# Two long-lived buffer pools of an attention and gated-MLP kernel change places in SBUF

## The chip, the core and the metric

The kernel runs on one core of one Trainium2 chip. The metric is device time in microseconds (us) of one execution, lower is better. The kernel before the change took 1835.28 us (median of 3 runs, 1833.83 to 1836.11).

## The reference

Three layers in a row on 4,608 tokens of width 512, all in float32. First an attention whose keys and values are averaged over groups of 8 positions, then a gated MLP, then an MLP with a rational function in place of the usual activation:

```
k_p, v_p = mean over groups of 8 rows of k, v            # 576 -> 72 per head
attn     = softmax(q @ k_p.T / 8);  x = attn @ v_p        # 8 batches, 8 heads, 64 wide
g        = x @ w_gate;  y = (silu(g) * (x @ w_val)) @ w_out      # 512 -> 1536 -> 512
h        = y @ w_in                                       # 512 -> 2048
P        = a0 + a1 h + a2 h^2 + a3 h^3
Q        = 1 + |b0| |h| + |b1| h^2
out      = (P / (Q + 1e-6)) @ w_out2                      # 2048 -> 512
```

## The kernel before, in words

A float32 operand is kept as two halves, a rounded `fp32r` part and the remainder, 512 columns each, side by side in one tile of 4,096 bytes a partition. A product is then three matmuls of 128x128 by 128x512 into one PSUM bank: high by high, low by high, high by low (`mm3`, L256, and the loop at L1081). Every matmul has a weight load of its own (a 128x128 stationary operand) in front of it, which TensorE runs while the matmul before it streams its 512 columns (the moving operand).

Tokens are worked on in nine blocks of 512. The work has four stages:

1. Blocks 0 to 2 of the gated MLP, a block for each outer turn (`gp` and `vp`: weights stationary, tokens `x` moving; `acc`: `w_out` stationary, the hidden tile `ht` moving). Attention for the blocks to come is put in between. In the first turn the weights are still being converted from their raw form.
2. Blocks 3 to 8 in three pairs, by a scheme of seven products in place of eight (`ca`, `cb`, `cc`, 36 turns). Weights and weight sums are streamed from HBM into slots (`sw`), the tokens' sums and differences lie in slots too (`x0t`, `x0b` and so on).
3. The output product of these pairs (L1081, `ya`, `yb`, `yc`). The weights (`oa`, `os`) lie in slots. The moving tiles go round a ring of seven: four tiles of the long-lived pool, then three slots (`ring_tile`).
4. The second MLP (L1110 on): 9 blocks of 16 turns. In a turn twelve matmuls `h` (weights `wi` stationary, tokens `z` moving) and then twelve matmuls `acco` of the turn two before (hidden tile `gt` stationary, weights `wo` moving). Of the token tiles `z` those of even blocks lie in slots and those of odd blocks in the long-lived pool (the last argument of `convert_x`).

The order of the instructions on each engine is written out by hand (`manual_schedule`); the pools decide addresses only. A tile pool takes the next free bytes of each partition when it is opened, so the order in which pools are opened sets where they lie. Two pools matter here:

- `wp`: 36 slots of 4,096 bytes, 147,456 bytes in all, a multiple of 256 (`wslot`).
- `keep`: five small tiles (`ident`, `vmask`, `cab`, `neg`, `lnb`), which take 640 bytes together, then four token tiles `x0` to `x3` of 4,096 bytes and `xraw` of 8,192 bytes.

The pools that are opened later (`hp` with `ht`; in the second MLP `p2` with `gt`) begin behind both.

Of the kernel before, what the change touches and what calls it, by code (L numbers as in the profile page):

```python
# [63 lines left out]
def attention_gated_rational(  # L64
# [3 lines left out]
):  # L68
    nc = tc.nc
    ctx.enter_context(tc.manual_schedule())  # L70
    wp = ctx.enter_context(tc.tile_pool(name="wp", bufs=WSLOTS))
    keep = ctx.enter_context(tc.tile_pool(name="keep", bufs=1))
    dram = ctx.enter_context(tc.tile_pool(name="dram", bufs=1, space=DRAM))
    ps_acc = ctx.enter_context(tc.tile_pool(name="ps_acc", bufs=4, space=PSUM))
    ps_gv = ctx.enter_context(tc.tile_pool(name="ps_gv", bufs=2, space=PSUM))
# [1162 lines left out]
```

## Time and profile before

| | |
|---|---|
| median of 3 runs | 1835.28 us |
| span of the profiled execution | 1834.7 us |
| TensorE matmul busy | 1772.9 us (97%) |
| VectorE busy | 1403.0 us (76%) |
| ScalarE busy | 1135.3 us (62%) |
| GpSimd busy | 342.8 us (19%) |
| matmuls of 128x512 | 7,020 of 8,212 |

The span is from the first to the last instruction of one profiled execution. The engine names of the rows are PE (TensorE matmul), PEld (TensorE weight load), DVE (VectorE), ACT (ScalarE), POOL (GpSimd) and SP (SyncE). The duration of one matmul in the profile (some 390 ns) runs from its start to its modelled end and overlaps the next one; what one costs in a stream is the distance between starts. Where a text speaks of the pitch, it means that distance: the time from the start of one run of matmuls to the start of the next, over their number.

### The profile page before, as it was taken

What the parts mean: (1) busy time and instruction counts of PE and PEld (TensorE: products, weight loads), DVE (VectorE), ACT (ScalarE), POOL (GpSimd) and SP (SyncE); (2) the same over time, 40 slices, a digit from 0 to 9 for tenths busy, and PEclk for the clock granted to TensorE, in tenths of its full rate; (3) what the DMA queues carried; (4) which work ended last, traced back from release to release, by engine and by line L of the source; (5) the groups of instructions that cost most, each with busy time, mean ns of one, the idle gap of its engine ahead of it and who ended that gap; (6) DMA issues with size and microseconds to landing.
All of it is one profiled execution on the core that took longest, in us unless ns stands there. A gap on an engine that the chain in (4) does not pass through costs nothing.

```text
span 1834.7 us, 23841 instructions
## 1 busy us (share of the span) xinstructions
PE 1772.9 (97%) x8212; PEld 1425.9 (78%) x8212; DVE 1403.0 (76%) x2333; ACT 1135.3 (62%) x1994; POOL 342.8 (19%) x492
## 2 busy tenths in 40 slices
PE   5899999999999999999999999999999999999998
PEld 4677877787777788777888788888888888888887
DVE  6996665558678666546777898889888989898987
ACT  5676455547665665435455666676667766776675
POOL 2343555442354344210000000000000000000000
PEclk9999999999999999999999999999999999999999
DMA  6531756659999788999826601010101010101000
GB/s 248 207 115 51 236 168 233 195 183 330 353 327 346 281 327 294 326 364 362 318 106 229 241 1 46 1 46 1 46 1 46 1 46 1 46 1 46 1 24 23
DMA packets 157464, 285.27 MB, mean 155 GB/s; under 512 B 12320, under 2 KB 78496, under 8 KB 156320
## 3 DMA queue, kind: packets, MB, share of 16 engines
q1 hardware_dynamic: 156624, 283.43, 44.1%
q8 instruction: 65, 1.06, 0.2%
q10 hardware_dynamic: 720, 0.33, 0.1%
q14 instruction: 55, 0.45, 0.1%
HBM read 194.58 MB, written 89.13 MB: 155 GB/s over the span
## 4 chain that ended last, share of the span: by engine, by line
PE 61%; DMA 1%; DVE 1%; ACT 0%; issue 0%; POOL 0%; SPq 0%; DVEq 0%; ACTq 0%
PE acco L256 22%; PE h L256 21%; PE ya L1081 5%; PE ca L256 4%; PE yc L1081 3%; PE cc L256 2%; PE yb L1081 1%; PE cb L256 1%; DMA sw<-wd 0%; DMA hl<-h 0%; PE pv L457 0%; DMA os<-so 0%; POOL t L722 0%; PE sc L368 0%; DVE gt L1169 0%
## 5 line engine op out<-in xcount | busy, mean ns | idle before, releaser
L256 PE MATMUL acco<-wo,gt 128*128 128x512 f32 x1728 | 426.6, 395 | 2.7 <-ACT gt L1168 2.2
L256 PE MATMUL h<-z,wi 128*128 128x512 f32 x1728 | 422.5, 393 | 0.0
L256 PEld LDWEIGHTS acco<-wo,gt 128*128 128x128 f32 x1728 | 324.9, 188 | 80.9 <-ACT gt L1168 3.1
L256 PEld LDWEIGHTS h<-z,wi 128*128 128x128 f32 x1728 | 324.3, 188 | 75.7
L1147 ACT ACTIVATE sq<-h 128x512 f32<-128x512 f32 x144 | 86.1, 598 | 221.6 <-PE h L256 221.4
L1154 DVE SCALAR_TENSOR_TENSOR w<-sq,neg,w 128x512 f32<-128x512 f32 x144 | 108.2, 751 | 66.9 <-ACT w L1148 62.4
L256 PE MATMUL vp<-x,wv 128*128 128x512 f32 x432 | 111.7, 406 | 5.9 <-DVE wv L149 5.9
L1164 DVE SCALAR_TENSOR_TENSOR g<-t,neg,e 128x512 f32<-128x512 f32 x144 | 108.2, 752 | 5.1
L1151 ACT ACTIVATE t<-h,neg 128x512 f32<-128x512 f32 x144 | 112.0, 778 | 0.0
L256 PE MATMUL gp<-x,wg 128*128 128x512 f32 x432 | 109.4, 400 | 2.6 <-DVE wg L149 2.6
L1160 DVE SCALAR_TENSOR_TENSOR t<-t,neg,h 128x512 f32<-128x512 f32 x144 | 107.7, 748 | 5.1
L1161 DVE SCALAR_TENSOR_TENSOR e<-w,ln 128x512 f32<-128x512 f32 x144 | 98.7, 686 | 13.5 <-ACT ln L1158 13.4
L256 PE MATMUL acc<-ht,wo 128*128 128x512 f32 x432 | 107.5, 398 | 0.0
L1158 ACT ACTIVATE ln<-ln,lnb 128x512 f32<-128x512 f32 x144 | 104.2, 724 | 4.7
L1162 DVE SCALAR_TENSOR_TENSOR e<-e,ln 128x512 f32<-128x512 f32 x144 | 99.7, 692 | 5.0
L1168 ACT ACTIVATE gt<-g 128x512 fp32r<-128x512 f32 x144 | 91.0, 632 | 16.8 <-DVE g L1164 16.8
L256 PEld LDWEIGHTS vp<-x,wv 128*128 128x128 f32 x432 | 81.0, 192 | 26.2 <-DVE wv L149 8.5
L1169 DVE TENSOR_TENSOR gt<-g,gt 128x512 fp32r<-128x512 f32 x144 | 98.8, 686 | 1.5 <-ACT gt L1168 0.8
L1148 ACT ACTIVATE w<-h,cab 128x512 f32<-128x512 f32 x144 | 98.3, 683 | 2.5 <-DVE e L1161 2.4
L1159 DVE TENSOR_TENSOR t<-t,h 128x512 f32<-128x512 f32 x144 | 98.2, 682 | 0.0
L256 PEld LDWEIGHTS gp<-x,wg 128*128 128x128 f32 x432 | 79.4, 188 | 23.3 <-DVE wg L149 4.7
L256 PEld LDWEIGHTS acc<-ht,wo 128*128 128x128 f32 x432 | 81.2, 190 | 18.5
(247 smaller groups left out, 3164.1 us busy)
## 6 DMA issues: line engine op xcount, KB each, us to landing
sw<-sd SPq DMA_DIRECT2D x72, 512.0 KB, 7.4
sw<-wd SPq DMA_DIRECT2D x36, 512.0 KB, 5.9
h<-hq SPq DMA_DIRECT2D x36, 512.0 KB, 6.5
sd<-sp SPq DMA_DIRECT2D x24, 512.0 KB, 4.1
sw<-vd SPq DMA_DIRECT2D x36, 256.0 KB, 7.7
hl<-h SPq DMA_DIRECT2D x18, 512.0 KB, 7.0
hr<-h SPq DMA_DIRECT2D x18, 512.0 KB, 9.9
out<-ob SPq DMA_DIRECT2D x36, 256.0 KB, 2.4
```

Of the source, the lines that this page charges most:

```text
L256: nc.tensor.matmul(acc, st[:, lw, cols], mv[:, rw, mcols], start=first and i == 0, stop=last and i == n - 1, skip_group_check=seeded,)
L1081: nc.tensor.matmul(banks[q], w[:, lw, cols], t[:, rw, :], start=opened and k == 0 and m == 0, stop=k == NK - 1 and m == 2, skip_group_chec ...
L1148: nc.scalar.activation(w0, hps, AF.Abs, scale=cab[:, 4:5])
L1151: nc.scalar.activation(t, hps, AF.Identity, scale=neg[:, 3:4], bias=neg[:, 2:3])
L1154: nc.vector.scalar_tensor_tensor(w0, sq, neg[:, 5:6], w0, op0=ALU.mult, op1=ALU.add)
L1158: nc.scalar.activation(ln, ln, AF.Exp, scale=-1.0, bias=lnb)
L1159: nc.vector.tensor_tensor(t, t, hps, op=ALU.mult)
L1160: nc.vector.scalar_tensor_tensor(t, t, neg[:, 1:2], hps, op0=ALU.add, op1=ALU.mult)
L1161: nc.vector.scalar_tensor_tensor(e, w0, C1, ln, op0=ALU.add, op1=ALU.mult)
L1162: nc.vector.scalar_tensor_tensor(e, e, 2.0, ln, op0=ALU.subtract, op1=ALU.mult)
L1164: nc.vector.scalar_tensor_tensor(g, t, neg[:, 0:1], e, op0=ALU.add, op1=ALU.mult)
L1169: lambda gt=gt, g=g: nc.vector.tensor_tensor(gt[:, 1, :], g, f32(gt[:, 0, :]), op=ALU.subtract),
```

## The change

Two lines change places, so that `keep` is opened first and `wp` second:

```diff
     nc = tc.nc
     ctx.enter_context(tc.manual_schedule())
+    keep = ctx.enter_context(tc.tile_pool(name="keep", bufs=1))
     wp = ctx.enter_context(tc.tile_pool(name="wp", bufs=WSLOTS))
-    keep = ctx.enter_context(tc.tile_pool(name="keep", bufs=1))
     dram = ctx.enter_context(tc.tile_pool(name="dram", bufs=1, space=DRAM))
```

No instruction is added, removed or moved: the order on all five engines is the same in both programs, row for row. What differs is the byte of a partition at which tiles begin, here in the built programs:

| tiles | before | modulo 256 | after | modulo 256 |
|---|---|---|---|---|
| slots of `wp` | 1,152 + 4,096 i | 128 | 26,368 + 4,096 i | 0 |
| `x0` to `x3` of `keep` | 149,248 + 4,096 i | 0 | 1,792 + 4,096 i | 0 |
| `xraw` of `keep` | 165,632 | 0 | 18,176 | 0 |
| `ident` of `keep` | 148,608 | 128 | 1,152 | 128 |
| `ht` and `cq` | 188,160 and 192,256 | 0 | the same | 0 |
| `gt` (second MLP) | 186,112 and 190,208 | 0 | the same | 0 |
| all other tiles of later pools | from 173,824 on | | the same | |

The low half of a pair begins 2,048 bytes into its tile, and a stationary operand is cut out of its tile at multiples of 512 bytes, so both halves and all cuts of a tile have the tile's byte modulo 256. Before the change a matmul's two operands so begin either at the same byte modulo 256 (slot with slot), or 128 bytes apart (slot with anything else). After it all 7,020 matmuls of 128x512 have both operands at 0 modulo 256. The smaller matmuls of the attention have operands in pools that don't move, but for block 0, whose attention tiles lie in slots.

## Rows read from the trace of the kernel before

**Rows 1.** The page: span, and busy time of each engine.

```profile
span 1834.7 us, 23841 instructions
PE 1772.9 (97%) x8212; PEld 1425.9 (78%) x8212; DVE 1403.0 (76%) x2333; ACT 1135.3 (62%) x1994; POOL 342.8 (19%) x492
```

**Rows 2.** Stretches: attention start, first MLP's three blocks, pairs, their output, second MLP.

```profile
core 0: us, PE busy (x) PEld busy (x) DVE busy (x) ACT busy (x) POOL busy (x), PEclk, DMA share, GB/s
39.70:176.80 137.10, 122.29 (x580) 93.83 (x579) 125.23 (x219) 98.71 (x164) 55.63 (x57) 0.98 0.33 114
176.80:293.60 116.80, 114.98 (x573) 92.71 (x573) 72.57 (x137) 55.95 (x107) 62.39 (x103) 1.00 0.63 202
293.60:424.00 130.40, 127.94 (x692) 102.30 (x691) 72.35 (x137) 66.21 (x101) 62.95 (x104) 1.00 0.63 211
424.00:848.80 424.80, 409.82 (x2025) 328.44 (x2024) 269.57 (x525) 246.54 (x468) 149.90 (x207) 0.99 0.94 332
848.80:1025.00 176.20, 174.63 (x757) 141.82 (x756) 131.37 (x215) 88.72 (x156) 0.00 (x0) 1.00 0.68 241
1025.00:1834.67 809.67, 803.33 (x3457) 649.03 (x3455) 706.03 (x1042) 559.03 (x935) 0.00 (x0) 1.00 0.08 29
```

**Rows 3.** What TensorE waited for in the whole span: us in total, times, longest.

```profile
PE vp L256 <- DVE wv L149: 5.9, 6, 1.8
PE t L429 <- POOL p L404: 5.8, 4, 2.2
...
PE ca L256 <- DMA sw<-wd: 2.7, 2, 1.8
PE gp L256 <- DVE wg L149: 2.6, 5, 1.0
PE acco L256 <- ACT gt L1168: 2.2, 2, 1.3
```

**Rows 4.** Timeline of TensorE from 856 us: start, duration, operation, out<-in, count.

```profile
856.24 2.90 PE L1081 MATMUL ya<-h0b,oa 128*128 128x512 f32 x12
858.98 1.52 PE L1081 MATMUL yc<-h0t,os 128*128 128x512 f32 x6
...
860.34 5.75 PE L1081 MATMUL yc<-h0t,os 128*128 128x512 f32 x24
...
865.93 1.54 PE L1081 MATMUL yc<-h0t,os 128*128 128x512 f32 x6
```

**Rows 5.** Timeline of TensorE among the pairs, from 729 us.

```profile
729.81 1.52 PE L256 MATMUL cc<-x2t,sw 128*128 128x512 f32 x6
731.17 1.52 PE L256 MATMUL ca<-x2t,sw 128*128 128x512 f32 x6
732.53 1.52 PE L256 MATMUL ca<-x1t,sw 128*128 128x512 f32 x6
```

**Rows 6.** Timeline of TensorE in the first MLP's third block.

```profile
400.45 2.95 PE L256 MATMUL acc<-ht,wo 128*128 128x512 f32 x12
403.23 2.96 PE L256 MATMUL gp<-x,wg 128*128 128x512 f32 x12
406.02 2.95 PE L256 MATMUL vp<-x,wv 128*128 128x512 f32 x12
408.81 1.55 PE L256 MATMUL acc<-ht,wo 128*128 128x512 f32 x6
```

**Rows 7.** The chain that ended last, second MLP, block 1: turns 11 apart.

```profile
1135.21 2.80 PE acco L256 x12
...
1196.73 2.80 PE acco L256 x12
```

**Rows 8.** Timeline of TensorE in the second MLP's block 2: turns, 13 apart at last.

```profile
1210.48 2.92 PE L256 MATMUL h<-z,wi 128*128 128x512 f32 x12
1213.24 2.96 PE L256 MATMUL acco<-wo,gt 128*128 128x512 f32 x12
1216.04 2.92 PE L256 MATMUL h<-z,wi 128*128 128x512 f32 x12
...
1282.68 2.92 PE L256 MATMUL h<-z,wi 128*128 128x512 f32 x12
```

**Rows 9.** The same timeline, the last five matmuls of one run alone.

```profile
1212.10 1.30 PE L256 MATMUL h<-z,wi 128*128 128x512 f32 x5
```

**Rows 10.** VectorE by line in the second MLP: busy us, mean ns, idle before.

```profile
L1164 DVE SCALAR_TENSOR_TENSOR g<-t,neg,e 128x512 f32<-128x512 f32 x144 | 108.2, 752 | 5.1
L1154 DVE SCALAR_TENSOR_TENSOR w<-sq,neg,w 128x512 f32<-128x512 f32 x144 | 108.2, 751 | 66.9 <-ACT w L1148 62.4
...
L94 DVE TENSOR_TENSOR z<-yraw,z 128x512 fp32r<-128x512 f32 x34 | 23.2, 684 | 0.3 <-ACT z L93 0.3
```

**Rows 11.** The splits of the tokens `z`: ns min/median/max, first and last start.

```profile
L94 DVE TENSOR_TENSOR z<-yraw,z x36: 681/684/693, 1023.3 to 1726.5; 128x512 fp32r<-128x512 f32 x36
L93 ACT ACTIVATE z<-yraw x36: 613/614/634, 1022.7 to 1724.1; 128x512 fp32r<-128x512 f32 x36
```

## The prediction

> **What bounds the kernel now.** I read the page's busy times first, then the stretches by stage, then TensorE's waits, and last its timeline, at places where the two operands of a matmul lie differently. TensorE is busy 1772.9 us of a span of 1834.7 [rows 1]; by stretches it is 98% in the second and third block of the first MLP, 96% among the pairs, and 99% in their output and in the second MLP, which alone has 809.67 us [rows 2]. Only in the first block (39.70 to 176.80 us) another engine presses: VectorE is busy 125.23 of 137.10 us there, TensorE 122.29, and the waits of `vp` and `gp` for converted weights, 5.9 and 2.6 us, belong to it [rows 2, 3]. All waits shown are small beside the span. So the kernel's time is the number of matmuls times their pitch, and the question is whether the pitch depends on where operands begin.
>
> It does, and the kernel before holds both cases next to each other. In the output of the pairs the stationary tile is always a slot (128 modulo 256), and the moving tile goes round a ring of four long-lived tiles (0) and three slots (128), six matmuls a tile. From 856.24 to 860.34 us stand 18 matmuls slot with slot: 4.10 us, 227.8 ns each. From 860.34 to 865.93 stand 24 matmuls slot with long-lived tile: 5.59 us, 232.9 ns each [rows 4]. Engine, line, shapes and weights are the same. Two other stages agree: among the pairs, slot with slot, six matmuls take 1.36 us, 226.7 ns each [rows 5] (the starts are rounded to 0.01 us, which is 0.6 ns on 18 matmuls; I work with 227.5 for alike operands and 233 for unlike ones); in the first MLP, where the operands begin 128 bytes apart, 36 matmuls take 408.81 - 400.45 = 8.36 us, 232.2 ns each [rows 6].
>
> The second MLP has `acco` always 128 apart (`gt` at 0, `wo` at 128), and `h` apart in odd blocks, alike in even ones. An odd block takes (1196.73 - 1135.21) / 11 = 5.593 us a turn, 233 ns a matmul [rows 7], an even one (1282.68 - 1210.48) / 13 = 5.554 us [rows 8]. In an even block a run of `h` takes 2.76 us, 230 ns each, more than 227.5. But the run's first seven take 1212.10 - 1210.48 = 1.62 us, 231 ns each, and its last five, up to the `acco` at 1213.24, 1.14 us, 228 each [rows 8, 9]: it comes out of an unlike run and needs some matmuls to settle. With `acco` alike too I expect both to stay settled.
>
> **The change part by part.** Nothing is added or moved in time; each edit is a shift of addresses. I go by what becomes of the pairs of operands, with 227.5 ns as the pitch of a pair that begins alike.
>
> - Second MLP, 3,456 matmuls. A turn of 24 becomes 24 x 227.5 = 5.460 us. Even blocks (0, 2, 4, 6, 8) have 80 turns: 80 x (5.554 - 5.460) = 7.5 us. Odd ones have 64: 64 x (5.593 - 5.460) = 8.5 us. Together 16.0 us. Bounds: at the 226.7 ns of [rows 5] a turn is 5.441 us and the gain 18.8; if the pitch stays at the 230 of the even blocks' `h`, a turn is 5.52 us and the gain 7.4. I take 227.5, between the two rows of alike operands [rows 4, 5].
> - Output of the pairs, 756 matmuls, 18 stretches of 24 with a long-lived tile: 432 x (233 - 227.5) = 2.4 us. The other 324 are alike before and after.
> - The pairs, 1,512 matmuls: slot with slot before and after, 0.
> - First MLP, blocks 1 and 2, 864 matmuls: 864 x (232.2 - 227.5) = 4.1 us, of which 98%, TensorE's busy share, comes through: 4.0.
> - First MLP, block 0, 432 matmuls: 2.0 us if all came through, nothing if VectorE with its 91% sets the pace. I take 0.6, nearer to the second, because of the waits for converted weights [rows 2, 3].
> - Attention of block 0, whose tiles lie in slots: its 24 transposes go from alike to unlike (`ident` stays at 128), and so do 16 products with `vs`; 16 others become alike. At 5.5 ns, and twice that since a plain float32 matmul shows as two, this is 0 to 0.5 us lost; I take 0.3.
> - VectorE, ScalarE and the DMAs. The splits of `z` write slots in even blocks and long-lived tiles in odd ones, and all 36 take 681 to 693 ns on VectorE and 613 to 634 on ScalarE [rows 11], so for these engines I take 0. Loads into slots now begin at 0 instead of 128; all that TensorE waits for streamed slots is 2.7 us [rows 3], so the most to be gained is 2.7; to be lost I see nothing in the rows but some added wait, which I set to the same 2.7. I take 0.
>
> Sum: 16.0 + 2.4 + 4.0 + 0.6 - 0.3 = 22.7 us. The profiled execution goes from 1834.7 to 1812.0 us. The median of the runs is 0.6 us above that span, so I predict 1812.5 us, 1.2% less.
>
> What is late next? In the second MLP VectorE. Seven operations a turn, of 682 to 752 ns [rows 10], come to some 5.0 us of the 5.46; a split of `z` makes it 5.7 in 32 of the 144 turns. Before each turn's `w` VectorE now sits idle 66.9 / 144 = 0.46 us, waiting for ScalarE, which waits for TensorE [rows 10]. That leaves it room of a third of a microsecond a turn, and `gt` is only wanted two turns later, so the long turns are made up for.
>
> **Rivals.**
>
> *VectorE takes over in the second MLP.* If the 32 turns with a split could not be made up for, each would cost 5.68 - 5.46 = 0.22 us, 7 us in all: 1819 to 1820 us. For it speaks VectorE's share, 706 of 810 us [rows 2]. Against it speaks that these turns are over 5.55 us already now, and TensorE waited for `gt` only twice, 2.2 us [rows 3].
>
> *Addresses don't matter, and the two pitches come from something else* that goes round with the ring, such as which tile was written shortly before. Then nothing changes: 1835 us. The block-wise difference in the second MLP, where tiles are written long before, speaks against it, and so does the first MLP, where `x` is as old as the block.
> The Trainium skill, in "SBUF — State Buffer", section "Who interferes with whom", states the same outcome as a rule: "PE and ACT never wait on anyone", and "TensorE: Matmul & The Clock Gate", section "What happens when you issue a matmul", says that loading the next weights takes no read bandwidth from the running matmul. By these pages the operands' place could not show, and the time would be this rival's. The trace does not agree: two pitches, 5.5 ns apart, with the same shapes and engines [rows 4].
>
> *It is byte 0 that costs, not the distance* (slower). The trace has pairs at 128 with 128 (fast), 128 with 0 and 0 with 128 (both slow), but no 512-column pair at 0 with 0, which is what all become. If any operand at 0 modulo 256 costs 5.5 ns once, all matmuls go to 233: even turns lose 0.038 us (3.0 in 80), the output of the pairs 324 x 5.5 = 1.8, the pairs 1,512 x 5.5 = 8.3, in all 13 us: 1848 us. If each operand at 0 costs it, the pitch is 238.5: 22 us lost in the second MLP, 6 in the output, 17 among the pairs, 8 in the first MLP, 53 in all: 1888 us. The change is a loss from a pitch of about 231 ns for 0 with 0, where the losses of the alike matmuls eat the gains of the others. Against it: weight load and moving stream read the same memory at the same time, and their distance is a plain reason for the one to hold up the other, while a start at a round address is a poor reason for being slow. That a run of `h` needs seven matmuls to settle also looks like two streams that fall into step.
>
> **How the numbers follow.** My forecast has 81%, VectorE taking over 8%, no effect 5%, byte 0 6%. What this kernel's measurement can tell from no change is about 0.2%, 3.7 us. The first two are both faster by more than that: faster 0.89, same 0.05, slower 0.06. The forecast's own bounds: with 226.7 ns everywhere (18.8 + 2.7 + 7.1 in the first MLP) and the 2.7 us of waits for streams, 31 us less, 1804; with the second MLP at 230 ns (7.4) and 2.4 + 2.0, and nothing in block 0, 12 us less, 1823. VectorE's rival lies in between. Range 1804 to 1823 us.
>
> **What would show it.** In the changed profile the ring of the output would show one pitch, 24 + 18 matmuls in 9.55 us where they now take 9.69; turns of even and odd blocks in the second MLP would both last 5.46 us; the runs among the pairs would stay at 1.36 us for six. The forecast is wrong if 0 with 0 shows 233 ns or more in the pairs, whose operands were alike before; if the ring keeps two pitches; or if the pitch falls and VectorE's idle time before `w` goes to nothing while TensorE waits for `gt`.

## The result, and the profile after

The changed kernel takes 1811.74 us (median of 4 runs, 1810.03 to 1811.98), the kernel before 1834.55 us in the same comparison (median of 4, 1832.36 to 1836.11). The ratio is 0.9866, 95% interval 0.9853 to 0.9879: 1.3% faster. The forecast was 1812.5 us, in a range of 1804 to 1823.

The span of the profiled execution fell from 1834.7 to 1809.9 us, 24.8 us; the medians of the runs are 22.8 us apart. The stages below are of one profiled execution of each kernel. Busy times first, of the page after: only TensorE's matmuls changed, by the same 24.8 us; the weight loads and the other engines do the same work in nearly the same time as in [rows 1].

```profile
span 1809.9 us, 23841 instructions
PE 1748.1 (97%) x8212; PEld 1426.2 (79%) x8212; DVE 1403.7 (78%) x2333; ACT 1135.4 (63%) x1994; POOL 344.0 (19%) x492
```

Then the stretches, cut at the same instructions as in [rows 2] (start and length; busy us and count of PE, PEld, DVE, ACT, POOL; granted TensorE clock; DMA share and GB/s):

```profile
38.50:175.60 137.10, 121.04 (x581) 93.78 (x581) 125.22 (x219) 98.61 (x164) 55.64 (x57) 0.98 0.33 114
175.60:290.80 115.20, 113.02 (x574) 92.47 (x573) 72.97 (x137) 55.87 (x107) 62.32 (x103) 1.00 0.64 205
290.80:420.00 129.20, 126.42 (x691) 102.15 (x690) 73.03 (x138) 66.81 (x101) 63.01 (x104) 1.00 0.62 213
420.00:845.20 425.20, 411.53 (x2025) 329.47 (x2024) 269.21 (x524) 246.14 (x467) 151.05 (x207) 0.98 0.94 332
845.20:1018.40 173.20, 171.61 (x757) 141.96 (x756) 131.27 (x214) 88.27 (x155) 0.00 (x0) 1.00 0.67 245
1018.40:1809.90 791.50, 784.99 (x3457) 648.84 (x3456) 706.33 (x1042) 559.54 (x936) 0.00 (x0) 1.00 0.08 30
```

The gain sits where the matmuls had unlike operands, and above all in the second MLP. The granted clock of the last three stretches is the same before and after, to 0.01:

| stretch | forecast gain, us | measured, us |
|---|---|---|
| start, attention of block 0 | -0.3 | 39.7 - 38.5 = 1.2 |
| first MLP, block 0 | 0.6 | 137.1 - 137.1 = 0.0 |
| first MLP, blocks 1 and 2 | 4.0 | 1.6 + 1.2 = 2.8 |
| pairs | 0 | 424.8 - 425.2 = -0.4 |
| output of the pairs | 2.4 | 176.2 - 173.2 = 3.0 |
| second MLP | 16.0 | 809.7 - 791.5 = 18.2 |
| sum | 22.7 | 24.8 |

The timeline of TensorE shows the pitch. In the output of the pairs, where [rows 4] have 227.8 and 232.9 ns in turn, each token's 36 matmuls now take 8.16 us whatever tiles of the ring they hold, 226.7 ns each:

```profile
855.24 8.32 PE L1081 MATMUL yc<-h0t,os 128*128 128x512 f32 x36
863.40 8.32 PE L1081 MATMUL ya<-h0t,os 128*128 128x512 f32 x36
```

In the second MLP every turn takes 5.44 us, in the even block 2 as here and in the odd block 1 alike; [rows 8] have 5.55, [rows 7] 5.59. Each run of twelve takes 2.72 us, `h` and `acco` alike; nothing is left of the run that has to settle [rows 9]:

```profile
1205.37 2.88 PE L256 MATMUL h<-z,wi 128*128 128x512 f32 x12
1208.09 2.88 PE L256 MATMUL acco<-wo,gt 128*128 128x512 f32 x12
1210.81 2.88 PE L256 MATMUL h<-z,wi 128*128 128x512 f32 x12
```

The first MLP's third block, against [rows 6]: 2.76 + 2.72 + 2.72 = 8.20 us for 36 matmuls, 227.8 ns each, 232.2 before:

```profile
396.93 2.93 PE L256 MATMUL acc<-ht,wo 128*128 128x512 f32 x12
399.69 2.88 PE L256 MATMUL gp<-x,wg 128*128 128x512 f32 x12
402.41 2.88 PE L256 MATMUL vp<-x,wv 128*128 128x512 f32 x12
405.13 1.07 PE L256 MATMUL acc<-ht,wo 128*128 128x512 f32 x4
```

And among the pairs, whose operands were alike before, six still take 1.36 us as in [rows 5], now at 0 with 0 instead of 128 with 128:

```profile
727.25 1.52 PE L256 MATMUL cc<-x2t,sw 128*128 128x512 f32 x6
728.61 1.52 PE L256 MATMUL ca<-x2t,sw 128*128 128x512 f32 x6
```

### The profile page after: what moved, and what is told of

Same layout as the page of the kernel before. It is cut to its first block, busy times and chain, and to the rows that moved or that the text cites. A ratio compares the mean times of both kernels' runs of the same rounds, so it can differ in the third digit from the quotient of the medians.

```text
span 1809.9 us, 23841 instructions
## 1 busy us (share of the span) xinstructions
PE 1748.1 (97%) x8212; PEld 1426.2 (79%) x8212; DVE 1403.7 (78%) x2333; ACT 1135.4 (63%) x1994; POOL 344.0 (19%) x492
## 4 chain that ended last, share of the span: by engine, by line
PE 59%; DMA 2%; DVE 1%; ACT 0%; issue 0%; POOL 0%; SPq 0%; DVEq 0%; ACTq 0%
PE h L256 21%; PE acco L256 21%; PE ya L1081 5%; PE ca L256 4%; PE yc L1081 3%; PE cc L256 2%; PE yb L1081 1%; PE cb L256 1%; DMA os<-so 1%; DMA sw<-wd 0%; DMA sw<-vd 0%; DMA hl<-h 0%; PE pv L457 0%; POOL t L722 0%; DVE gt L1169 0%
## 5 line engine op out<-in xcount | busy, mean ns | idle before, releaser
L256 PE MATMUL acco<-wo,gt 128*128 128x512 f32 x1728 | 415.8, 390 | 2.8 <-ACT gt L1168 2.4
L256 PE MATMUL h<-z,wi 128*128 128x512 f32 x1728 | 415.0, 390 | 0.0
L1154 DVE SCALAR_TENSOR_TENSOR w<-sq,neg,w 128x512 f32<-128x512 f32 x144 | 108.0, 750 | 47.8 <-ACT w L1148 47.8
L256 PEld LDWEIGHTS gp<-x,wg 128*128 128x128 f32 x432 | 79.3, 188 | 22.7 <-DVE wg L149 5.1
```

The lines of the kernel that those rows point to most:

```text
L256: nc.tensor.matmul(acc, st[:, lw, cols], mv[:, rw, mcols], start=first and i == 0, stop=last and i == n - 1, skip_group_check=seeded,)
L1154: nc.vector.scalar_tensor_tensor(w0, sq, neg[:, 5:6], w0, op0=ALU.mult, op1=ALU.add)
```

## Experiments

"Apart" means: at another byte modulo 256. The sweeps, the shift of the moving operand and the kernels with alternating matmuls have one run each; the kernel before took 1833.6 to 1835.3 us beside them, and only their pitches are read, not their times.

### One part undone: the token tiles apart

```diff
     ident = keep.tile([P, P], F32, name="ident")
+    x_first = [keep.tile([P, 2, BLK], F32R, tag=f"x{kk}", name=f"x0_{kk}") for kk in range(KT)]
     vmask = keep.tile([P, 4], F32, name="vmask")
...
-    x = [keep.tile([P, 2, BLK], F32R, tag=f"x{kk}", name=f"x0_{kk}") for kk in range(KT)]
+    x = x_first
```

> The changed kernel, with the four small tiles of the long-lived pool placed behind its token tiles, so that the token tiles x0 to x3 alone lie 128 bytes (modulo 256) away from the slots; ht and gt stay alike with the slots. Theory (the distance of a matmul's two operands modulo 256 sets its pitch): the ring in the output of the pairs shows two pitches again, 233 and 227 ns; among the second MLP's turns those of odd blocks take about 5.55 us, those of even blocks stay at 5.44; the first MLP loses about 2 us; in all some 12 us slower than the changed kernel, about 1824 us. Rival (any operand that begins at 0 modulo 256 was the point, or the new place of the pools as such): no stage differs between odd and even blocks, 1812 us.

Measured: 1820.62 us (5 runs; ratio to before 0.9926, 0.9913 to 0.9938), about 9 us of the gain lost where 12 were expected. The ring shows two pitches again, as expected. From 857.38 to 862.97 us stand 24 matmuls with long-lived tiles, 232.9 ns each; the first slot behind them takes 1.38 us for six, and the next two slots are at 226.7 ns:

```profile
857.38 5.75 PE L1082 MATMUL yc<-h0t,os 128*128 128x512 f32 x24
862.97 1.54 PE L1082 MATMUL yc<-h0t,os 128*128 128x512 f32 x6
864.35 2.88 PE L1082 MATMUL ya<-h0t,os 128*128 128x512 f32 x12
```

Timeline of TensorE in the odd block 1: a turn takes 1121.96 - 1116.43 = 5.53 us, the run of `h` 2.79 us, that of `acco` 2.74.

```profile
1116.43 2.95 PE L257 MATMUL h<-z,wi 128*128 128x512 f32 x12
1119.22 2.90 PE L257 MATMUL acco<-wo,gt 128*128 128x512 f32 x12
1121.96 2.96 PE L257 MATMUL h<-z,wi 128*128 128x512 f32 x12
...
1207.41 2.88 PE L257 MATMUL acco<-wo,gt 128*128 128x512 f32 x12
...
1212.85 2.88 PE L257 MATMUL acco<-wo,gt 128*128 128x512 f32 x12
```

In the even block 2 a turn stays at 1212.85 - 1207.41 = 5.44 us. So moving only `x0` to `x3` brings back the slow stages that use these tiles, and no others: the odd blocks (5.5 us in 64 turns), the output of the pairs (176.2 us, as before the change) and blocks 1 and 2 of the first MLP (2.0 us). The place of the pools as such has no part in it. The odd turns are a little shorter than the 5.55 us expected, since `acco` after an unlike `h` is hardly disturbed (2.74 against 2.72 us), while [rows 8] showed `h` after an unlike `acco` at 2.76. That accounts for some 1.5 of the missing 3 us; the rest is not traced, and single executions differ by as much.

### The other part undone: the hidden tiles apart

```diff
     wp = ctx.enter_context(tc.tile_pool(name="wp", bufs=WSLOTS))
+    few = ctx.enter_context(tc.tile_pool(name="few", bufs=1))
...
-    vmask = keep.tile([P, 4], F32, name="vmask")
+    vmask = few.tile([P, 4], F32, name="vmask")      # cab, neg and lnb too
```

> The changed kernel, with the four small tiles in a pool of their own behind the slots. Slots and token tiles then begin at 128 modulo 256, alike; ht and gt begin at 0, 128 bytes away. Theory of the distance: the ring has one pitch of 227 ns although its operands now lie at 128; every turn of the second MLP takes 5.55 us, as an even block's did before the change, 144 x 0.114 = 16 us; acc of the first MLP loses 1 to 2 us; in all about 1829 us. Rival (the byte itself matters, 128 or 0): the ring has another pitch than in the changed kernel, 233 ns, and the output of the pairs takes 2 to 4 us longer.

Measured: 1826.86 us (5 runs; ratio 0.9958, 0.9944 to 0.9971), 15 us of the gain lost, 17 expected. Timeline: a token of the ring, now at 128 with 128, takes 861.19 - 853.03 = 8.16 us, just as at 0 with 0; a turn of the second MLP takes 1123.72 - 1118.17 = 5.55 us, as expected.

```profile
853.03 8.32 PE L1082 MATMUL yc<-h0t,os 128*128 128x512 f32 x36
861.19 1.07 PE L1082 MATMUL ya<-h0t,os 128*128 128x512 f32 x4
...
1118.17 2.92 PE L257 MATMUL h<-z,wi 128*128 128x512 f32 x12
1120.92 2.96 PE L257 MATMUL acco<-wo,gt 128*128 128x512 f32 x12
1123.72 2.92 PE L257 MATMUL h<-z,wi 128*128 128x512 f32 x12
```

The byte itself plays no part that shows: 0 with 0 and 128 with 128 have one pitch. The rival "byte 0 costs" is shown wrong, by this run and by the pairs of the changed kernel.

### Which distances are slow: three sweeps

In the changed kernel's second MLP the hidden tile gets eight buffers, each at its own distance; a run of twelve `acco` has one distance.

```diff
-            gt = p2.tile([P, 2, BLK], F32R, tag="gt", name=f"gt{n}", bufs=2)
+            off = (0, 8, 16, 24, 32, 40, 48, 56)[n % 8]
+            gt = p2.tile([P, 2 * BLK + 64], F32R, tag=f"gt{n % 8}", name=f"gt{n}")
+            gt = gt[:, off : off + 2 * BLK].rearrange("p (t c) -> p t c", t=2)
```

> The changed kernel with eight buffers for the hidden tile gt of the second MLP instead of two, the first byte of each at another distance from the slots: 0, 32, 64, 96, 128, 160, 192 and 224 modulo 256, used in turn. Each run of twelve acco then has one distance, 18 turns each. Theory A (two streams that read the same memory and hold each other up, by distance): some distances give 227 ns, 128 gives 233, and those in between go over by degrees, or one of them is better than 227. Rival B (only equal beginnings are fast): 0 gives 227, the other seven about 233. Rival C (only which half of the 256 bytes): 32 to 96 like 0, 128 to 224 like 128.

> The same as the sweep before with the distances 4, 256, 8, 272, 48, 400, 240 and 336 bytes modulo 512. Theory (modulo 256): 256 is like 0, 227 ns. Rival (a larger modulus, 512): 256 is slower than 0, 230 ns or more. The small distances 4, 8, 16 show whether alike means the same byte or the same line of some width: the same line gives 227, the same byte 230 or more.

> The sweep with eight buffers for gt once more, now with odd multiples of 16 bytes: 144, 272, 16, 496, 112, 432, 80 and 464 modulo 512, most in another buffer than before. The two sweeps so far found 0, 256, 272, 240 and 400 at 226.7 ns and all else at 229 to 234, so equal beginnings are not the only fast ones. If the distance modulo 256 alone decides, whatever the buffer: 144 is 226.7 as 400 was, 16 and 272 are 226.7, 496 is 226.7 as 240 was, 80 is 231.7 as 336 was; 112, 176 (432) and 208 (464) are new. If instead the buffer or its place modulo 512 did it, some of these come out the other way.

Measured, from the starts of the runs of `acco` (17 or 18 runs of each, without the first of a sweep, which holds a wait; stationary less moving operand, modulo 256):

```
bytes apart   0     4     8     16    32    48    64    80    96    112
ns a matmul   226.7 231.7 231.0 226.7 232.8 232.8 233.2 231.7 234.0 233.0

bytes apart   128   144   160   176   192   208   224   240
ns a matmul   233.0 226.7 233.2 229.9 229.0 231.5 232.6 226.7
```

Rows of the second sweep's timeline; the runs of `acco` have 4 bytes (2.78 us to the start of the next `h`), 256 (2.72) and 400, that is 144 modulo 256 (2.72):

```profile
1116.14 2.94 PE L256 MATMUL acco<-wo,gt 128*128 128x512 f32 x12
1118.92 2.91 PE L256 MATMUL h<-z,wi 128*128 128x512 f32 x12
1121.66 2.88 PE L256 MATMUL acco<-wo,gt 128*128 128x512 f32 x12
1124.38 2.88 PE L256 MATMUL h<-z,wi 128*128 128x512 f32 x12
...
1143.56 2.88 PE L256 MATMUL acco<-wo,gt 128*128 128x512 f32 x12
1146.28 2.88 PE L256 MATMUL h<-z,wi 128*128 128x512 f32 x12
```

What follows. 256 is as good as 0, so nothing here asks for a modulus larger than 256. The distances that were tried in two buffers or modulo 512 (16, 80, 144, 240) agree to 0.1 ns: the distance decides, not the buffer. But equal beginnings are not the only fast ones, as the second theory of the first sweep had it: 16, 144 and 240 reach the same 226.7 ns, 176 and 192 lie between, and a shift of 4 bytes costs nearly as much as 128. None of the three theories of the first sweep fits the table, which doesn't rise by degrees and isn't split in halves. No distance tried goes under 226.7 ns, so the sweeps offer no better place for the pools than the changed kernel's.

### The moving operand shifted instead

```diff
     ident = keep.tile([P, P], F32, name="ident")
+    x_first = [token(0)]                   # token(kk) allocates tile x<kk> of keep
+    for kk in range(1, KT):
+        keep.tile([P, 8], F32, name=f"pad{kk}")
+        x_first.append(token(kk))
     vmask = keep.tile([P, 4], F32, name="vmask")
...
-    x = [keep.tile([P, 2, BLK], F32R, tag=f"x{kk}", name=f"x0_{kk}") for kk in range(KT)]
+    x = x_first
```

> The changed kernel with the four token tiles of the long-lived pool in steps of 32 bytes: their beginnings lie 32, 64, 96 and 128 bytes behind that of the slots (x0: 32, x1: 64, x2: 96, x3: 128, modulo 256), slots and gt alike. Here the moving operand is the one that is shifted, where the sweeps shifted the stationary one. In the ring of the output each tile has six matmuls in a row. If the distance (stationary less moving) decides whichever operand is shifted: x0 (224) 232.6 ns, x1 (192) 229, x2 (160) 233.2, x3 (128) 233, the three slots 227, as in the first sweep. Rival (a moving operand is judged by another rule than a stationary one): another order of these, such as all four at the same value.

Measured, in the ring (18 stretches of six each, medians): x0 (224 apart) 233.7 ns, x1 (192) 228.8, x2 (160) 235.0, x3 (128) 233.3, and of the slots the first 229.2, the other two 226.7. One round of the four, from start to start 1.40, 1.37, 1.41 and 1.40 us (the next starts at 865.21):

```profile
859.63 1.56 PE L1089 MATMUL yc<-h0t,os 128*128 128x512 f32 x6
861.03 1.53 PE L1089 MATMUL yc<-h0t,os 128*128 128x512 f32 x6
862.40 1.57 PE L1089 MATMUL yc<-h0t,os 128*128 128x512 f32 x6
863.81 1.56 PE L1089 MATMUL yc<-h0t,os 128*128 128x512 f32 x6
```

Each is within 2 ns of the sweep's value for its distance, with 192 the lowest and 160 the highest both times; 224 and 128, which lie close together, change places. The sign counts: `x1` begins 64 bytes behind the slots and is as fast as 192 in the sweep (229.0), not as slow as 64 (233.2). For the pitch itself it makes no great difference which of the two operands is shifted. The slots begin at 96 modulo 256 in this kernel, a third byte at which alike pairs take 226.7 ns.

### Own operands or the next weights?

A weight load runs while the matmul before it streams: in the changed kernel loads of 1426.2 us and matmuls of 1748.1 us fit into a span of 1809.9. So the stream may meet the load of the *next* matmul's weights, and in runs of twelve these have the same distance as its own. To part them, the matmuls of `h` and `acco` were issued in turn, one by one, with `acco` three turns behind (and four buffers for `gt` in place of two):

```diff
-        LAG = 2
+        LAG = 3
...
-            hps = hidden(j, f)
-            if n >= LAG:
-                out2(*its[n - LAG])
...
+                hps = hidden(j, f, ones)               # collects the matmuls
+                out2(*its[n - LAG], twos)
+                for one, two in zip(ones, twos):
+                    for args, flags in (one, two):
+                        nc.tensor.matmul(*args, **flags)
```

The pools of the second experiment (hidden tiles apart), so that `h` is alike in itself and apart from the next weights, and `acco` the other way round:

> The kernel with hidden tiles apart, with the matmuls of the second MLP's turns in another order: one of h, one of acco, in turn, in place of twelve and twelve, and acco three turns behind in place of two. All moving operands of the second MLP (z, wo) begin at 128 modulo 256; of the stationary ones wi begins at 128 and gt at 0. So each matmul's own pair is alike in h and apart in acco, but the weights that are loaded while it streams (the next matmul's) are apart in h and alike in acco. Theory (it is the load of the next weights that meets the stream): a start to start of h is 231 to 236 ns, one of acco 224 to 228. Rival (a matmul's own two operands): the other way round. If both come out alike, the two can't be told apart in this way.

Measured: means of 233.6 ns from a start of `h` to the next, 230.8 from one of `acco` (odd blocks, starts under 260 ns apart). The first is as the theory had it, the second is not, and the pair takes 464.4 ns (a turn 5.57 us), nearly as much as two matmuls apart (466). It leans to the next weights, but a delay in one matmul can show in the next, so it settles nothing. Hence a case in which all matmuls of a block are of one kind:

> The kernel before, its pools in the old order, with the matmuls of the second MLP's turns one of h and one of acco in turn, acco three turns behind. In odd blocks z and gt begin at 0 and both weights at 128 modulo 256: every matmul's own two operands are 128 apart, but the weights that are loaded while it streams, the next matmul's, are alike with it (z with gt, wo with wi). Theory (the load of the next weights meets the stream): odd blocks take 24 x 226.7 = 5.44 us a turn, although no matmul's own operands are alike; even blocks, where z lies at 128 and so meets the load of gt, stay at the 5.57 us that the kernel with hidden tiles apart took in this order. Rival (a matmul's own two operands): odd blocks 24 x 233 = 5.59 us or more, longer than even ones.

> The same order of matmuls with the changed kernel's pools, where all operands begin at 0 modulo 256: the control for the order itself. Both theories: 5.44 us a turn in odd and even blocks alike. If a turn takes longer here, alternating costs something by itself, and that has to come off the other run's turns.

And the reverse of it, for four turns in each block:

```diff
+        MOVED = range(6, 10)
+        for f in MOVED:                       # wo of these turns, 128 bytes further on
+            far = p2.tile([P, 2 * BLK + 64], F32R, name=f"far{f}")
+            far = far[:, 32 : 32 + 2 * BLK].rearrange("p (t c) -> p t c", t=2)
+            nc.sync.dma_start(f32(far), second.kept[f"o2_{f}"])
+            W2[f"o2_{f}"] = far
...
+            off = 32 if f in MOVED else 0     # and gt of these turns
```

> The control of the alternating order (all operands at 0 modulo 256, 5.44 us a turn), with gt and wo of four of the sixteen acco in each block (the 7th to 10th) moved to 128 modulo 256. These four stand in the turns of the 10th to 13th h, whose z and wi stay at 0. In these turns every matmul's own two operands are alike, but the weights loaded while it streams are 128 apart from it (z at 0 with gt at 128, wo at 128 with wi at 0): the reverse of the odd blocks of the earlier alternating run, which took 5.52 us, neither the 5.44 of all alike nor the 5.59 of all apart. If the next weights alone decide, these turns take about 5.59 us; if a matmul's own two operands alone decide, 5.44; if both have a share, as 5.52 hints, about 5.5 once more.

As whole kernels these four are slower: 1854.0, 1861.7, 1839.8 and 1842.9 us. In each, one turn near the start of every block but the first takes 8.2 to 9.9 us; there `acco` waits for ScalarE's copies into `ob` (19.9 us in all in the control). Those turns are left out here.

The turns can be read off ScalarE's first operation of each (`sq`, which waits for `h`). The kernel before in this order, odd block 1, own operands apart, next weights alike: 5.52 us.

```profile
1160.39 0.60 ACT L1155 ACTIVATE sq<-h 128x512 f32<-128x512 f32 x1 [1.88 <-PE h L1149]
1165.91 0.60 ACT L1155 ACTIVATE sq<-h 128x512 f32<-128x512 f32 x1 [1.88 <-PE h L1149]
```

The control, all alike: 5.44 us.

```profile
1159.93 0.60 ACT L1155 ACTIVATE sq<-h 128x512 f32<-128x512 f32 x1 [1.28 <-PE h L1149]
1165.37 0.60 ACT L1155 ACTIVATE sq<-h 128x512 f32<-128x512 f32 x1 [1.80 <-PE h L1149]
```

The last kernel, own operands alike, next weights apart, in the turns of the 11th to 13th `h` of block 1: 5.48 us (the 10th, the first with moved operands, takes 5.50). The 14th turn, all alike again, also takes 5.48: its first eight matmuls average 231.5 ns, the other sixteen 226.7. The 15th takes 5.44.

```profile
1161.38 0.60 ACT L1161 ACTIVATE sq<-h 128x512 f32<-128x512 f32 x1 [1.32 <-PE h L1155]
1166.86 0.60 ACT L1161 ACTIVATE sq<-h 128x512 f32<-128x512 f32 x1 [1.84 <-PE h L1155]
...
1172.34 0.60 ACT L1161 ACTIVATE sq<-h 128x512 f32<-128x512 f32 x1 [1.32 <-PE h L1155]
1177.82 0.60 ACT L1161 ACTIVATE sq<-h 128x512 f32<-128x512 f32 x1 [1.32 <-PE h L1155]
1183.26 0.60 ACT L1161 ACTIVATE sq<-h 128x512 f32<-128x512 f32 x1 [1.28 <-PE h L1155]
```

```
a turn of 24, us         next weights alike   next weights apart
own operands alike       5.44                 5.48
own operands apart       5.52                 5.59 (kernel before, runs of twelve)
```

Neither theory gives these numbers: by the next weights alone the lower left would be 5.44 and the upper right 5.59, by a matmul's own operands the reverse. So a matmul's own two operands are not all that counts: with these alone at fault the upper right would be 5.44. The two costs don't add up matmul by matmul, though. By the table, unlike own operands would cost 3.3 ns a matmul and unlike neighbours 1.7, and a turn in which `h` has the one and `acco` the other would take 5.50 us. Such turns are those of the first alternating kernel and the even blocks of the second, and they take 5.57, here in even block 2 of the second:

```profile
1275.78 0.60 ACT L1155 ACTIVATE sq<-h 128x512 f32<-128x512 f32 x1 [1.41 <-PE h L1149]
1281.35 0.60 ACT L1155 ACTIVATE sq<-h 128x512 f32<-128x512 f32 x1 [1.41 <-PE h L1149]
```

What a distance costs hangs on the matmuls before it too, as the slow first matmuls of the 14th turn above show. And in the upper right cell the weights and the moving operand of the matmul *before* are 128 bytes away as well, so that it is the next weights among these is argued, not shown. All four cells in one order of matmuls were not run either.

## Why the prediction was right

**What bounds the kernel.** Right: TensorE's busy time and the span fell by the same 24.8 us, and no other engine's time changed by more than 1.2.

**The pitch.** Right in kind, and the gain a little low. Alike pairs were put at 227.5 ns, between the two rows; in the changed kernel they take 226.7 (5.44 us / 24), the value that the forecast kept as its bound. For the second MLP that bound gave 18.8 us, the forecast 16.0, and 18.2 were measured. The row that pulled the value up was the 227.8 of [rows 4]: its 18 matmuls begin with the first slot behind the long-lived tiles, where six still take 857.62 - 856.24 = 1.38 us, 230 ns each; the other twelve, up to 860.34, take 226.7 (the second row is cut off by its window):

```profile
856.24 1.54 PE L1081 MATMUL ya<-h0b,oa 128*128 128x512 f32 x6
857.62 1.30 PE L1081 MATMUL ya<-h0b,oa 128*128 128x512 f32 x5
```

So the settling that the forecast saw in `h` was in the ring too, and was counted there as pitch. At 226.7 the term of the output of the pairs is 2.7 us instead of 2.4; the rest of the 3.0 measured is this first slot (229.2 ns before, 226.7 after), which the forecast took to be the same before and after.

**The total.** That 22.7 us were forecast and the medians differ by 22.8 is in part luck. The profiled pair differs by 24.8; the second MLP, the output and the start gave 4.3 us more than forecast, the other stages 2.2 less. And the start, block 0 and the pairs vary from execution to execution: over the twelve traces of this case the start takes 38.3 to 39.9 us, the block 135.6 to 138.2 and the pairs 423.0 to 427.0.

**The settling of runs.** Right: with `acco` alike, `h` has no slow first matmuls any more, and odd and even blocks are equal.

**The first MLP.** Block 0 gained nothing; the forecast's 0.6 allowed for a little coming through past VectorE, which is busy 125.2 of 137.1 us before and after. A gain of that size could not be seen in one execution of each. Blocks 1 and 2 gave 2.8 us of 4.0: the term was sized by a stretch without attention. One part went into longer waits of the attention's transposes for VectorE. In the two blocks these are now, in us, times and longest

```profile
PE t L429 <- DVE p L379: 3.0, 4, 1.3
PE t L433 <- DVE p L379: 1.5, 7, 0.2
PE t L429 <- POOL r L637: 0.4, 1, 0.4
```

in all 4.9 us, where the kernel before had 2.7 + 1.1 + 0.3 = 4.1. When TensorE gets there earlier and the softmax doesn't, the time turns into waiting. The other 0.4 us (1.1, if the term is worked out with 226.7 ns) are not traced to a cause.

**The start.** 0.3 us of loss were forecast, 1.2 of gain measured. 0.9 of that is one wait for the first load of `q`, 5.5 us before and 4.6 after. It is 5.5 and 5.6 us in the two traces with the old order of the pools and 4.1 to 5.1 in the ten with `keep` first, so it may have to do with the change; two traces are too few to tell. The price put on block 0's attention was a little high: its transposes show as one matmul each, only the products as two, so at 5.5 ns it is 0.3 us at most and not 0.5.

**What is late next.** VectorE did not take over. Its idle time before `w` in the second MLP fell from 66.9 us [rows 10] to 47.8, a third of a microsecond a turn as forecast, and TensorE's waits for `gt` stayed at two, 2.4 us, 2.2 before [rows 3]:

```profile
L1154 DVE SCALAR_TENSOR_TENSOR w<-sq,neg,w 128x512 f32<-128x512 f32 x144 | 108.0, 750 | 47.8 <-ACT w L1148 47.8
```

**The rivals.** "Addresses don't matter" is refuted by the two runs in which only small tiles moved past others, and "byte 0 costs" by 0 with 0 at 226.7 ns. What the forecast used, that alike operands are fast, held. Its reason, two streams that read the same memory side by side, is not shown: the sweeps and the table of own and next operands tell that distance matters, not which read waits for which. What the forecast quoted from the Trainium skill ("SBUF — State Buffer", section "Who interferes with whom": "PE and ACT never wait on anyone") would have made the first rival's time. The measured time, 1811.74 us against 1834.55, does not agree with that.

## What to carry to other kernels

Where TensorE is the bound, compare the pitch of the same matmul at several places of the timeline; two values with the same shapes, steady over many turns, are worth a look at the addresses. With float32 pairs in tiles that are a multiple of 256 bytes, it is enough to let the pools of stationary and moving tiles begin at the same byte modulo 256, by putting odd-sized small tiles ahead of all of them; here that was worth 1.3% without touching an instruction. Of the first block, where VectorE is busy 91% of the time, none of the gain could be seen.

## What the runs showed of the hardware

- The pitch of a 128x512 matmul with a weight load of its own is 226.7 ns at a granted clock of 1.00 with alike operands, and up to 235 ns by the distance of their addresses (stationary less moving, modulo 256). 4 bytes of distance cost 5.0 ns.
- The dependence on distance is not by degrees: 16, 144 and 240 bytes are free, 32 to 128 cost 5 to 7 ns, 192 costs 2.3. I have no rule for it.
- A matmul's own two operands are not all that counts: with these alike, but the operands of its neighbours 128 bytes away, a turn takes 5.48 us against 5.44.
- Alike matmuls behind unlike ones can need seven or eight to settle [rows 8, 9], and it depends on the distance: in the sweeps the twelve `h` behind a run of `acco` average 230.2 ns after 112 or 128 bytes, 229.2 after 64 and 226.7 to 226.9 after 8, 32, 48 or 224.
